# Attention and a Fourier mixing layer on one core: turned tiles and attention's outputs go through memory in fewer transfers, the second batch's outputs too

## The chip, the core and the metric

The kernel runs on one core of a Trainium2 chip. The core has a matrix engine (TensorE, PE in the profile; PEld are its weight loads), three engines for everything else (VectorE or DVE, ScalarE or ACT, GpSimd or POOL), and a sequencer, SyncE or SP, which here only issues transfers. Transfers run on 16 DMA engines between memory and the core's SBUF; PE writes to a small memory of its own, PSUM, from which DVE and ACT read. The metric is the device time in microseconds of one execution, as the median of several runs; a profile of one execution comes with it.

## The reference

For 4 batches, 8 heads, 768 rows and 64 columns per head, attention with a block mask (blocks of 32 rows: neighbours, the first and last block, and three drawn blocks per block row), and after it a Fourier mixing layer on the joined heads (4 x 768 x 512):

```python
scores = scale * np.matmul(q, k.transpose(0, 1, 3, 2))
scores = np.where(mask, scores, -1000000000.0)
attn = exp(scores - max) ; attn = attn / (sum(attn) + 1e-09)
x = (attn @ v).transpose(0, 2, 1, 3).reshape(B, S, H * D)

X = np.fft.fft(np.fft.fft(x, axis=1), axis=2)
u = x + np.real(X)
un = (u - mean(u)) / np.sqrt(var(u) + 1e-06)
out = u + np.maximum(un @ w_ch1, 0.0) @ w_ch2      # 512 -> 2048 -> 512
```

## The kernel before

The work is laid out by a planner written in Python: it emits the instructions of all engines in one order, and each engine then runs its own in that order, waiting by semaphores for what an instruction needs. The planner keeps an estimate of each engine's time (`when`), and decides by it where a step goes.

**Attention** goes in *slots*. A pair of heads (16 pairs, 4 per batch) has 6 slots; a slot takes two units of 128 keys for one half of the queries (384). For each unit PE makes the scores (`scores`, L578); ACT takes the exponential, and PE multiplies it by v one slot later (`values`, L652), adding into the one PSUM buffer `o`. The mask comes in one of two ways. As long as no channel products are waiting, PE adds it into the scores (L588, four products to a slot) and ACT writes `e` itself (L598). Later, ACT works in place (L606) and DVE multiplies by the mask (L608). Row sums are collected by additions on DVE (L633) or POOL (L638) and taken up by PE (L733, `sp`).

**An output** `o` of a pair and a half is turned, so that rows come to lie in partitions, and put into `x`, the input of the mixing layer. There are two ways. `place`: ACT copies `o` to `oT` (L663), PE turns it in three products with the identity (L675, `xt`), ACT copies the result into `x` (L676). `place_blocks`: DVE turns `oT` in blocks of 32 x 32 (L660), and SP puts the 16 blocks in place with 16 transfers from SBUF to SBUF (L691). `in_blocks` says which pairs take the second way: before, all of batches 2 and 3 but the first pair of each. `sum_p` holds one `oT`.

**The mixing** of a batch (`fourier`, `mixer`) starts when its attention is done and runs beside the next batch's attention: folds on DVE, products along the rows (`zp`, L856) and across (`pq`, L887 to L904) on PE, then per tile of 128 rows and per half `arrive` (L926), `spread` (statistics, L937), `whiten` (L951), which gives the normalised `un`. For the channel products `un` must be turned. In the last batch PE does that (L992). In the others `un_blocks` turns blocks of 32 x 32 on DVE (L1010) and writes them to memory (`far`, L1013, four transfers per tile of 128 x 512); when all six tiles of a batch are there, `un_back` fetches both halves into `unT` (L1022, four transfers per half). `unT` has two buffers in all.

**The channel products** follow. `right` makes four differences of `unT` on DVE (L1053); a `quad` then is seven products of the first weight (`xp`, `yp`, `z`, L1091) with sums on DVE (L1096) and a ReLU on ACT (L1100); `channels` multiplies by the second weight (`y`, L1147), adds into `x` (L1150) and stores it (L1158). They make up the greater part of PE's work and are spread over the attention of the next batch.

**What sets the order.** Steps of the mixing wait in the queue `apart`, channel products in `late`, short PE steps (turnings, totals) in `short`. `gap` emits steps from `apart` as far as the planner's times allow. A step of `right` (kind `"b"`) is to wait until `state["back"]`, which `un_back` sets to the planner's time plus `BACK` (9.0 us). But at the end of each slot from batch 2's attention on, a loop takes up to four steps from `apart` regardless, when fewer than 18 are left:

```python
for _ in range(4 if phase > 1 and not late and len(apart) < 6 * T else 0):
    if apart and not late:
        do_apart()
```

When the last step of `apart` is emitted, the channel products become available and the mask goes over from PE to DVE (`masks["by_pe"] = False`).

All transfers here are issued by SP, in order: loads of q (L230), k (L230) and v (L270), block transfers, `far` writes, fetches, stores. An issue that waits holds up the others behind it.

Of the kernel before, what the change touches and what calls it, by code (L numbers as in the profile page):

```python
# [11 lines left out]
FP32 = mybir.dt.float32  # L12
# [10 lines left out]
def _words(ap, n):  # L23

    return bass.DRamTensorHandle(ap.tensor.name, (2 * n,), I32)
# [74 lines left out]
def kernel(  # L100
# [14 lines left out]
    nc = tc.nc  # L115

    B, H, S, D = q.shape
    DM = H * D
    FF = w_ch1.shape[1]
    P = 128  # L120
    C = S // P
    BLK = 32
    NB = S // BLK
    NR = sampled_blocks.shape[1]
    HS = S // 2
# [4 lines left out]
    T = C // 2  # L130
# [4 lines left out]
    NP = H // 2  # L135
# [40 lines left out]
    xp = ctx.enter_context(tc.tile_pool(name="xp", bufs=2))  # L176
# [8 lines left out]
    far_p = ctx.enter_context(tc.tile_pool(name="far_p", bufs=1, space=bass.MemoryType.DRAM))  # L185
# [7 lines left out]
    when = {"PE": 0.0, "ACT": 0.0, "DVE": 0.0, "POOL": 0.0}  # L193
    free = {"m": [0.0, 0.0], "t": [0.0]}

    def busy(engine, us, after=0.0):
        when[engine] = max(when[engine], after) + us
        return when[engine]

    def bank(tag):  # L200

        at = free[tag].index(min(free[tag]))
        when["PE"] = max(when["PE"], free[tag][at])
        free[tag][at] = float("inf")
        return tag, at

    def give(which, at):
        free[which[0]][which[1]] = at + HOP
# [91 lines left out]
    def bit(n):  # L300
# [5 lines left out]
                      in_=bass.AP(tensor=_words(sampled_blocks, NB * NR), offset=0,  # L306
                                  ap=[[0, NB], [1, 2 * NB * NR]]))
# [135 lines left out]
    for w, w_sb in ((w_ch1, w1_sb), (w_ch2, w2_sb)):  # L443
        rows, cols = w.shape
# [45 lines left out]
    turned, e_of, acc_of, o_of, sums_of, x_of, sp_of = {}, {}, {}, {}, {}, {}, {}  # L490
# [176 lines left out]
    def place(n, half):  # L667

        b, j = pairs[n]
        oT = o_of.pop((n, half))  # L670
        if j == 0:
            x_of[b, half] = xp.tile([P, T, DM], FP32, tag=("xA", "xB")[half], name="x")
        xt, at = ps_t.tile([P, 512], FP32, tag="t", name="xt"), bank("t")
        for c in range(T):
            nc.tensor.transpose(xt[:, c * P:(c + 1) * P], oT[:, c * P:(c + 1) * P], ident)  # L675
        nc.scalar.copy(out=x_of[b, half][:, :, j * P:(j + 1) * P],  # L676
                       in_=xt[:, 0:HS].rearrange("p (c f) -> p c f", c=T))
        give(at, busy("ACT", 0.5, busy("PE", 0.45, oT_at[n, half]) + HOP))

    def in_blocks(n):  # L680

        return n > 2 * NP and n % NP > 0

    def place_blocks(n, half):
        b, j = pairs[n]
        oT = o_of.pop((n, half)).rearrange("p (c t d) -> p c t d", t=P // BLK, d=BLK)
        for g in range(P // BLK):
            for t in range(P // BLK):  # L690
                nc.sync.dma_start(  # L691
                    out=x_of[b, half][BLK * t:BLK * t + BLK, :, j * P + BLK * g:j * P + BLK * (g + 1)],
                    in_=oT[BLK * g:BLK * g + BLK, :, t, :])

    def into_sums(key, j, sp):
        if j == 0:
# [281 lines left out]
    def mixer(b, xA, xB):  # L978


        uns, unT = {}, {}
# [21 lines left out]
        lines = {}  # L1003

        def un_blocks(half, m):

            un = uns.pop((half, m))
            if half not in lines:
                lines[half] = far_p.tile([BLK, DM // BLK, HS], FP32, tag=f"un{half}", name="far")
            nc.vector.transpose(out=un, in_=un)  # L1010
            for g in range(P // BLK):
                n = m * P + g * BLK
                nc.sync.dma_start(out=lines[half][:, :, n:n + BLK],  # L1013
                                  in_=un[BLK * g:BLK * g + BLK, :].rearrange(
                                      "j (t i) -> j t i", i=BLK))

        def un_back():

            for half in range(2):
                unT[half] = tr_p.tile([P, ND, T * P], FP32, tag="tr", name="unT")  # L1020
                for a in range(P // BLK):
                    nc.sync.dma_start(out=unT[half][BLK * a:BLK * a + BLK, :, :],  # L1022
                                      in_=lines[half].rearrange(
                                          "j (k a) n -> a j k n", a=P // BLK)[a])
            state["back"] = max(when["PE"], state["ready"]) + BACK

        t, s = {}, {}
        K1, K2 = slice(0, ND // 2), slice(ND // 2, ND)
# [169 lines left out]
        def outputs(r, m, after):  # L1198
# [60 lines left out]
            if r == 1:  # L1259
# [5 lines left out]
              for h in range(2)]  # L1265

        ft = [[("d", lambda h=h, m=m: un_blocks(h, m), 0.0, 0.0, 0.7) for m in range(T)]
              for h in range(2)]

# [9 lines left out]
        if not last:  # L1279
            before = first + [pq[1], ar[0][1], ar[1][1], sp[0][1],  # L1280
                              pq[2], wh[0][1], ft[0][1], ar[0][2], ar[1][2], sp[0][2],
                              pq[0], wh[0][2], ft[0][2], ar[0][0], ar[1][0], sp[0][0],
                              sp[1][1], wh[0][0], ft[0][0], sp[1][2], wh[1][1], ft[1][1],
                              sp[1][0], wh[1][2], ft[1][2], wh[1][0], ft[1][0]]
            after = ([("-", un_back, 0.0, 0.0, 0.0)] + le +
                     [("b", lambda i=i: right(i, 0, 1, 2), 0.0, 0.0, 1.0) for i in (1, 2, 3, 4)])
# [5 lines left out]
        for r in range(0 if last else NF // 4):  # L1292
# [9 lines left out]
    MOST, LEAST = 9.6, 2.5  # L1302
    COVER = 100.0
    AHEAD = 2.2
    BACK = 9.0
    ALONE = 3.0
    LEAVES = 9.0
    SP = UP // SLOT
# [2 lines left out]
    short, apart, late, due = deque(), deque(), deque(), deque()  # L1311
    asked = set()
    needed = set()
    state = {"paired": False, "total": None, "w": 0, "got": 0, "owed": 0.0, "ready": 0.0,
             "back": 0.0}
# [9 lines left out]
    def do_apart():  # L1325
        kind, fn, pe, act, dve, _ = apart.popleft()
        if kind[0] in "dwb":
            dve += behind(kind)
            state["ready"] = busy("DVE", dve, {"w": rstd_at[0] if rstd_at else 0.0,
                                               "b": state["back"]}.get(kind, state["ready"])) + HOP  # L1330
            fn()
            return
        done = state["ready"]
        if kind != "-":
            at = bank(kind[0])
            done = busy("PE", pe, done) + HOP
        fn()
        if act:
            done = busy("ACT", act, done) + HOP
        if dve:  # L1340
            done = busy("DVE", dve, done) + HOP
        if kind != "-":
            give(at, done - HOP)
        state["ready"] = done
# [31 lines left out]
    def until(met):  # L1376

        while not met():
            if late:
                channel_step()  # L1380
                gap(2.0)
            else:
                do_apart()
# [35 lines left out]
    def slot(sl):  # L1419
        phase, r = divmod(sl, SB)  # L1420
        n, s = divmod(sl, SP)
# [48 lines left out]
        if s >= (5 if reuse else 3) and (n, 0) in oT_at and once(n):  # L1470
            b, j = pairs[n]
            at = oT_at[n, 0]
            if reuse:
                until(lambda: (b - 2, 0) in finished)
                at = when["PE"] + LEAVES
            if in_blocks(n):
                place_blocks(n, 0)
            else:
                short.append(("t", at, lambda: place(n, 0)))
        if 0 < sl <= B * SB and s == 0 and n % NP != 1:  # L1480
            if in_blocks(n - 1):
                place_blocks(n - 1, 1)
            else:
                short.append(("t", oT_at[n - 1, 1], lambda: place(n - 1, 1)))
        if sl < B * SB and n % NP == 1 and s == 1:
            b = pairs[n - 1][0]
            at = oT_at[n - 1, 1]
            if b >= 2:
                until(lambda: (b - 2, 1) in finished)
                at = when["PE"] + LEAVES  # L1490
            short.append(("t", at, lambda: place(n - 1, 1)))
        if sl > SB and s == 0 and sl <= B * SB:
            short.append(("t", acc_at[n - 1, 1], lambda: total(n - 1)))
            state["total"] = short[-1]
# [27 lines left out]
            gap(rest())  # L1522

        for _ in range(4 if phase > 1 and not late and len(apart) < 6 * T else 0):
            if apart and not late:
                do_apart()

        must = (3, 5) if paired else (2, 5)
# [5 lines left out]
        while short and (not more or soon) and (  # L1534
                s in must or len(short) > 1 or phase == 0 or soon or sl == B * SB):
            ready = [i for i in short if max(i[1], min(free[i[0]])) <= when["PE"] + 0.1]
# [36 lines left out]
    for sl in range(B * SB + 1):  # L1573
        slot(sl)
        if sl == B * SB - 4:
            flag = highest()
        if sl == B * SB - 2:
            over = nc.values_load(flag[0:1, 0:1], min_val=0, max_val=1)
# [107 lines left out]
```

## Time and profile before

| | |
|---|---|
| median of 3 runs | 1062.29 us (1061.61 to 1062.72) |
| the profiled execution's own time | 1060.62 us |
| its span, first to last instruction | 1058.8 us |
| PE busy | 1022.0 us (97%), 4334 instructions |
| DVE busy | 677.8 us (64%), 1236 |
| ACT busy | 356.5 us (34%), 718 |
| POOL busy | 241.6 us (23%), 272 |
| granted PE clock, mean | 0.991 |
| transfers | 55.72 MB in 162,017 packets, 146,572 of them under 512 bytes |
| L675, turning of outputs on PE | 60 products of 128 x 128, 11.0 us busy |
| L588, mask on PE | 200 products, 24.9 us busy |
| L660, turning on DVE | 12, 584 ns each |
| far<-un | 72 issues of 64 KB |
| unT<-far | 24 issues of 192 KB |
| x<-oT | 192 issues of 12 KB |

A line of a timeline is: start in us, duration, engine, line of the kernel, operation, what it writes and reads, the shape, how many were merged, and in brackets the idle time of the engine before it and what ended it. Where a wait is put down to a transfer, the name is that of a transfer that landed at about that time, and may be another than the one waited for. Between about 123 and 264 us attention of batch 1 runs beside the mixing of batch 0; batch 0's channel products, with batch 1's mixing, fill most of 264 to 414; batch 2's attention starts with slot 48 at 226 us and is then spread to 557; batch 3's attention runs from 542 to 786.

### The profile page before, as it was taken

How to read it: one execution, taken by the hardware profiler on the slowest of the kernel's cores; microseconds unless marked ns; L12 is line 12 of the kernel's file. 1: busy time of each engine (PE TensorE's matmuls, PEld its weight loads, DVE VectorE, ACT ScalarE, POOL GpSimd, SP SyncE). 2: the span in 40 equal slices, each digit the busy share in tenths (PEclk: the TensorE clock that was granted, in tenths of full speed). 3: DMA queues.
4: the chain of work that ended last, by engine and by line, in shares of the span. 5: the costliest groups of instructions: out<-in, count | busy, mean ns of one | idle time of the engine just before them, and what ended most of it. 6: DMA issues, size and time to landing. Idle time of an engine off the chain costs nothing.

```text
span 1058.8 us, 12480 instructions
## 1 busy us (share of the span) xinstructions
PE 1022.0 (97%) x4334; PEld 529.7 (50%) x4334; DVE 677.8 (64%) x1236; ACT 356.5 (34%) x718; POOL 241.6 (23%) x272
## 2 busy tenths in 40 slices
PE   8999999987999999999999999899999999999996
PEld 4333345433465554444444654344444654578575
DVE  6898795968754845564578466665457364674663
ACT  6988755553120112342441210253220211210210
POOL 1000183554200100554553001255520001000000
PEclk9999999998999999999999999999999999999999
DMA  7757422381000124222230003621000001000001
GB/s 214 230 170 225 108 46 46 50 147 28 1 0 11 20 44 96 57 38 44 41 56 1 1 11 60 134 43 27 12 10 5 1 1 37 24 1 1 1 16 47
DMA packets 162017, 55.72 MB, mean 53 GB/s; under 512 B 146572, under 2 KB 155034, under 8 KB 161946
## 3 DMA queue, kind: packets, MB, share of 16 engines
q1 hardware_dynamic: 160694, 54.11, 22.7%
q10 hardware_dynamic: 1220, 0.72, 0.3%
q8 instruction: 36, 0.59, 0.2%
q14 instruction: 35, 0.29, 0.1%
q0 software_dynamic: 32, 0.01, 0.0%
HBM read 41.44 MB, written 11.01 MB: 50 GB/s over the span
## 4 chain that ended last, share of the span: by engine, by line
PE 82%; DVE 6%; DMA 3%; ACT 3%; SPq 2%; issue 2%; POOL 0%; ACTq 0%; DVEq 0%
PE y L1147 22%; PE z L1091 15%; PE s L578 11%; PE o L652 9%; PE yp L1091 7%; PE yy L1212 7%; PE xp L1091 4%; PE zp L856 2%; PE sp L719 1%; DVE t L1053 1%; ACT e L598 1%; DMA kb<-in_k_dram 1%; PE s L588 1%; DMA out_dram<-x 1%; PE sp L733 1%
## 5 line engine op out<-in xcount | busy, mean ns | idle before, releaser
L638 POOL TENSOR_TENSOR acc<-acc,e 128x384 f32<-128x384 f32 x162 | 164.6, 1052 | 97.4 <-DVE e L608 81.1
L578 PE MATMUL s<-qT,kT 64*128 64x384 f32 x768 | 156.5, 523 | 20.4 <-DVE e L608 13.1
L652 PE MATMUL o<-e,vr 128*64 128x384 f32 x768 | 142.4, 498 | 0.0
L1147 PE MATMUL y<-w_sb,hB 128*128 128x512 f32 x288 | 128.6, 597 | 0.3 <-DVE x L1150 0.3
L1147 PE MATMUL y<-w_sb,hA 128*128 128x512 f32 x288 | 127.9, 595 | 0.0
L1150 DVE TENSOR_TENSOR x<-y,x 128x512 f32<-128x512 f32 x72 | 49.7, 691 | 111.7 <-PE y L1147 111.6
L608 DVE TENSOR_TENSOR e<-s,mask 128x768 f32<-128x768 f32 x92 | 83.8, 951 | 58.1 <-ACT s L606 49.9
L578 PEld LDWEIGHTS s<-qT,kT 64*128 64x128 f32 x768 | 64.4, 187 | 100.1 <-DVE e L608 28.0
L638 POOL TENSOR_TENSOR acc<-e 128x384 f32<-128x384 f32 x44 | 48.5, 1123 | 257.3 <-PE sp L733 127.2
L606 ACT ACTIVATE s<-s 128x768 f32<-128x768 f32 x92 | 70.0, 792 | 92.6 <-PE s L578 92.4
L1091 PE MATMUL z<-unT,t 128*128 128x384 f32 x256 | 93.2, 487 | 0.7 <-DVE hA L1096 0.7
L598 ACT ACTIVATE e<-s 128x768 f32<-128x768 f32 x100 | 76.0, 810 | 48.6 <-PE s L588 29.6
L1147 PEld LDWEIGHTS y<-w_sb,hB 128*128 128x128 f32 x288 | 53.6, 191 | 67.2 <-issue 65.7
L1147 PEld LDWEIGHTS y<-w_sb,hA 128*128 128x128 f32 x288 | 53.7, 190 | 63.7 <-issue 60.2
L652 PEld LDWEIGHTS o<-e,vr 128*64 128x64 f32 x768 | 48.1, 137 | 71.5 <-issue 68.0
L1096 DVE TENSOR_TENSOR hA<-z,hA 128x384 f32<-128x384 f32 x64 | 35.7, 557 | 68.5 <-PE z L1091 68.5
L1100 ACT ACTIVATE hA<-hA 128x384 f32<-128x384 f32 x64 | 33.4, 523 | 123.8 <-DVE hA L1096 123.8
L1091 PEld LDWEIGHTS z<-unT,t 128*128 128x128 f32 x256 | 48.5, 190 | 35.4 <-DVE hA L1096 2.0
L1100 ACT ACTIVATE hB<-hB 128x384 f32<-128x384 f32 x64 | 33.5, 523 | 86.2 <-DVE hB L1096 83.8
L1111 ACT COPY hA<-xp 128x384 f32<-128x384 f32 x32 | 15.3, 478 | 128.6 <-PE xp L1091 128.6
L1091 PE MATMUL yp<-unT,w_sb 128*128 128x384 f32 x128 | 46.7, 487 | 0.8 <-ACT hA L1111 0.6
L1091 PE MATMUL xp<-unT,w_sb 128*128 128x384 f32 x128 | 47.2, 492 | 0.0
(208 smaller groups left out, 1364.2 us busy)
## 6 DMA issues: line engine op xcount, KB each, us to landing
wraw<-in_moe_w_ch_dram SPq DMA_DIRECT2D x32, 512.0 KB
vr<-in_v_dram SPq DMA_DIRECT2D x30, 192.0 KB
far<-un SPq DMA_DIRECT2D x72, 64.0 KB
unT<-far SPq DMA_DIRECT2D x24, 192.0 KB
qb<-in_q_dram SPq DMA_DIRECT2D x44, 96.0 KB
kb<-in_k_dram SPq DMA_DIRECT2D x44, 96.0 KB
x<-oT SPq DMA_DIRECT2D x192, 12.0 KB
out_dram<-x SPq DMA_DIRECT2D x11, 252.0 KB
```

The lines of the kernel that those rows point to most:

```text
L578: nc.tensor.matmul(s[:, i, 0:HS], kT[rows, c * P:(c + 1) * P], qT[rows, queries], start=True, stop=u not in by_pe)
L598: nc.scalar.activation(out=e, in_=s[:, :, 0:HS], func=ACT.Exp, scale=scale)
L606: nc.scalar.activation(out=s[:, :, 0:HS], in_=s[:, :, 0:HS], func=ACT.Exp, scale=scale)
L608: nc.vector.tensor_tensor(out=e, in0=s[:, :, 0:HS], in1=m.broadcast_to([P, 2, HS]), op=ALU.mult)
L638: nc.gpsimd.tensor_add(out=acc[:, i, :], in0=start[:, i, :], in1=e[:, i, :])
L652: nc.tensor.matmul(o[D * i:D * i + D, :], vt[:, i, c, :], e[:, i, :], start=(c == 0), stop=(c == C - 1))
L1091: nc.tensor.matmul(to, a[:, k, :], c[:, k, :], start=(k == 0), stop=(k == ND // 2 - 1))
L1096: tt(out=to, in0=ps, in1=a, op=ALU.add)
L1100: nc.scalar.activation(out=h, in_=h, func=ACT.Relu)
L1147: nc.tensor.matmul(y, hs[0, half][:, l, m * P:(m + 1) * P], w2_sb[:, 4 * r + l, :], start=(l == 0), stop=(l == 3))
L1150: nc.vector.tensor_tensor(out=x[:, m, :], in0=y, in1=x[:, m, :], op=ALU.add)
L1212: nc.tensor.matmul(ps, a[:, k, :], c[k // 2][:, k % 2, :] if isinstance(c, list) else c[:, k, :], start=(k == 0), stop=(k == 3))
```

## The change

- `in_blocks` now also holds for the four pairs of batch 1.
- `place_blocks` goes through memory: four transfers write the blocks of `oT` into a tile `row` in memory, in pieces of 128 bytes, and four read it into `x`, in pieces of 512 bytes. The four reads wait until the writes have landed.
- `un_blocks` writes a turned tile to memory as it is, in one transfer of 256 KB (2 KB per row). `un_back`, still in four transfers per half, does the rearrangement on its way back, in pieces of 128 bytes instead of 1,536; 8 x 1,536 = 12,288 pieces to a batch.
- `BACK` is 13.0 for batch 0 and 12.0 for the others.
- The loop at the end of a slot leaves a step of `right` in the queue until `state["back"]` is near.

```diff
-        return n > 2 * NP and n % NP > 0
+        return NP <= n and (n < 2 * NP or n % NP > 0)

     def place_blocks(n, half):
         b, j = pairs[n]
-        oT = o_of.pop((n, half)).rearrange("p (c t d) -> p c t d", t=P // BLK, d=BLK)
+        rows = far_p.tile([BLK, T, P // BLK, P], FP32, tag=f"oT{half}", name="row", bufs=2)
+        oT = o_of.pop((n, half))
         for g in range(P // BLK):
-            for t in range(P // BLK):
-                nc.sync.dma_start(
-                    out=x_of[b, half][BLK * t:BLK * t + BLK, :, j * P + BLK * g:j * P + BLK * (g + 1)],
-                    in_=oT[BLK * g:BLK * g + BLK, :, t, :])
+            nc.sync.dma_start(
+                out=rows.rearrange("r c t f -> r (c t) f")[:, :, BLK * g:BLK * g + BLK],
+                in_=oT[BLK * g:BLK * g + BLK, :].rearrange("r (ct d) -> r ct d", d=BLK))
+        if j == 0:
+            x_of[b, half] = xp.tile([P, T, DM], FP32, tag=("xA", "xB")[half], name="x")
+        for t in range(P // BLK):
+            nc.sync.dma_start(
+                out=x_of[b, half][BLK * t:BLK * t + BLK, :, j * P:(j + 1) * P],
+                in_=rows[:, :, t, :])
...
-                lines[half] = far_p.tile([BLK, DM // BLK, HS], FP32, tag=f"un{half}", name="far")
+                lines[half] = far_p.tile([T, P, DM], FP32, tag=f"un{half}", name="far")
             nc.vector.transpose(out=un, in_=un)
-            for g in range(P // BLK):
-                n = m * P + g * BLK
-                nc.sync.dma_start(out=lines[half][:, :, n:n + BLK],
-                                  in_=un[BLK * g:BLK * g + BLK, :].rearrange(
-                                      "j (t i) -> j t i", i=BLK))
+            nc.sync.dma_start(out=lines[half][m], in_=un)
...
+                of = lines[half].rearrange("m (g j) (k a i) -> a j k (m g) i",
+                                           j=BLK, a=P // BLK, i=BLK)
                 for a in range(P // BLK):
-                    nc.sync.dma_start(out=unT[half][BLK * a:BLK * a + BLK, :, :],
-                                      in_=lines[half].rearrange(
-                                          "j (k a) n -> a j k n", a=P // BLK)[a])
-            state["back"] = max(when["PE"], state["ready"]) + BACK
+                    nc.sync.dma_start(
+                        out=unT[half][BLK * a:BLK * a + BLK].rearrange(
+                            "j k (g i) -> j k g i", i=BLK),
+                        in_=of[a])
+            state["back"] = max(when["PE"], state["ready"]) + BACK[b > 0]
...
-    BACK = 9.0
+    BACK = 13.0, 12.0
...
-            short.append(("t", at, lambda: place(n - 1, 1)))
+            if in_blocks(n - 1):
+                place_blocks(n - 1, 1)
+            else:
+                short.append(("t", at, lambda: place(n - 1, 1)))
...
-            if apart and not late:
+            if apart and not late and (apart[0][0] != "b" or
+                                       state["back"] < max(when["DVE"], when["PE"]) + 0.2):
                 do_apart()
```

## The prediction

> **What bounds the kernel now.** I read the page's busy shares first: TensorE (PE) 1022.0 of 1058.8 us, the chain of waits 82% PE. A saving must therefore take work off PE or fill a place where PE stands. The PE timelines show the two places that matter. The first is where batch 0's normalised rows come back from memory:
>
> ```profile
> 229.58 1.56 PE L578 MATMUL s<-qT,kT 64*128 64x384 f32 x8
> 230.97 0.49 PE L588 MATMUL s<-factors 64*128 64x384 bf16 x4
> 231.39 0.55 PE L675 MATMUL xt<-ident,oT 128*128 128x128 f32 x3
> 231.87 1.51 PE L652 MATMUL o<-e,vr 128*64 128x384 f32 x8
> ...
> 245.32 2.93 PE L578 MATMUL s<-qT,kT 64*128 64x384 f32 x8 [8.08 <-DVE e L608]
> ```
>
> The reader sees one slot of attention (scores L578, mask L588, a turned output L675, outputs L652), then PE standing 8.08 us for VectorE (DVE). The DVE timeline says why: it stands at the fetched tile `unT`, with everything behind it.
>
> ```profile
> 226.16 0.95 DVE L633 TENSOR_TENSOR acc<-acc,e 128x768 f32<-128x768 f32 x1
> 236.96 1.11 DVE L1053 TENSOR_TENSOR t<-unT 128x768 f32<-128x768 f32 x1 [9.85 <-DMA kb<-in_k_dram]
> ```
>
> The second place is batch 2's (ACT, DVE and PE timelines):
>
> ```profile
> 662.31 0.48 ACT L676 COPY x<-xt 128x384 f32<-128x384 f32 x1 [17.97 <-DMA out_dram<-x]
> ```
>
> ```profile
> 676.03 1.82 DVE L1053 TENSOR_TENSOR t<-unT 128x768 f32<-128x768 f32 x1 [3.93 <-DMA kb<-in_k_dram]
> ```
>
> ```profile
> 657.18 1.56 PE L578 MATMUL s<-qT,kT 64*128 64x384 f32 x8
> 664.54 2.79 PE L578 MATMUL s<-qT,kT 64*128 64x384 f32 x8 [3.06 <-DVE e L608]
> ...
> 692.68 1.78 PE L578 MATMUL s<-qT,kT 64*128 64x384 f32 x8 [1.14 <-DVE e L608]
> ```
>
> ScalarE (ACT) cannot place an output because the store that frees the tile is late in SP's queue; the exponentials behind it are late, and PE stands. Last, windows over 140-171, 184-223, 246.5-248.5 and 228-234 us (busy us and count of PE, PE loads, DVE, ACT, POOL, then clock, DMA share, GB/s):
>
> ```profile
> 140.00:171.00 31.00, 29.86 (x181) 13.27 (x177) 30.34 (x31) 17.48 (x34) 20.04 (x17) 1.00 0.21 39
> 184.00:223.00 39.00, 36.99 (x231) 16.57 (x231) 37.33 (x65) 20.29 (x44) 22.44 (x24) 1.00 0.39 67
> 246.50:248.50 2.00, 2.00 (x9) 0.66 (x6) 0.59 (x1) 1.00 (x2) 2.00 (x3) 0.55 0.98 158
> 228.00:234.00 6.00, 6.00 (x43) 2.42 (x39) 0.00 (x0) 4.58 (x8) 3.13 (x4) 1.00 1.04 215
> ```
>
> DVE is full in the first two (30.34 of 31, 37.33 of 39): while batch 0 is mixed, it has no room. The last two give the rate of 128-byte pieces (a q load, 158 GB/s) and of 1,536-byte pieces (the fetch, 215), both into 32 partitions.
>
> **The change, part by part.** Sums go against the profiled execution's 1060.62 us; the median 1062.29 stands 1.67 above it.
>
> (1) Batch 1's eight outputs leave PE: 24 transposes. A slot with one starts 138.86 and ends 142.60 (3.74), one without 135.60 to 138.86 (3.26). 8 x 0.47 = **-3.8**. With them 8 copies of L663 (480 ns) and 8 of L676 (484 ns) leave ACT, 34% busy: 0.
>
> (2) The order of the changed program starts batch 0's channel products after attention's slot 53 instead of between 51 and 53, and the mask stays on PE until then: 16 more L588, four slots. A slot with masks takes 3.26, one without 2.93 (259.81 to 262.74): 4 x 0.33 = **+1.3**. For these, DVE makes 8 sums (1044 ns) instead of 8 mask products (951 ns), POOL 16 additions fewer: 0, DVE being idle there.
>
> (3) The right-hand tiles (L1053) are no longer pushed onto DVE before they can have come. The 8.08 goes, and the slow stretch behind it (granted clock 0.55 in the row above: 2.93 for 1.56, and 0.4 at 254.3): **-9.9**. Late next are (4) and (5).
>
> (4) The eight turnings move to DVE, 584 ns each (L660). PSUM has one buffer `o`, so PE's next half of outputs waits until DVE has read the last. ACT did this at once; DVE has a queue. Walk along the rows of before: the first turning stands behind L633, which ends 142.5, so it ends 143.1, where PE would start its next L652 at 140.7: 2.4. The third stands before the L545 at 167.5, with 1.96 of L826-L828 moved behind it and three turnings ahead, 1.75, and 0.4 of a wait for a sum: 167.7, where PE would be at 164.2: 3.5. In 184-223, DVE's 39.5 us get four turnings (2.3), one sum (1.0) and 2.4 in which it waits for the last products of z, which PE reaches only after such a wait: 45.2, against 38.3 of PE's ten slots: 7.0. Together 12.9, less the 3.5 of like waits that stand there already (L578 and L675 on ACT): **+9.4**. Bounds: 0, if DVE's lag costs no more than it does now, and 12.9. I take the walk, because DVE's 30.34 of 31 is nearest to it.
>
> (5) The new wait for the first fetch. On SP, the last normalised tile and the fetch now stand behind a k load (4 issues, 2.2), four row writes (2.6), their landing, four reads into x (2.6); then one write of 256 KB (0.6). A transfer's fixed part is the fetch's 10.45 (issue 226.51 to 236.96) less 1.573 MB at 215 GB/s (7.3): 3.1, so the landing costs 2.5 after the issue ends. The fetch itself is 12,288 pieces of 128 bytes, at 158 GB/s 10.0 plus 3.1. Sum 23.6, of which 2.0 runs before DVE's last turned tile; two L1053 follow (2.7): 24.3 after it. PE gets there 18.3 after it (five slots 17.2, xp and yp 2.9, less 1.8 that it was ahead). **+6.0**, the first channel product z behind it, nothing else on DVE. Bounds: 0 (k load and row hop hidden), and 10.3 (reads at half of 215).
>
> First stretch: -3.8 + 1.3 - 9.9 + 9.4 + 6.0 = **+3.0**.
>
> (6) Batch 2. The same stretch of batch 1 takes 27.33 (414.56 to 441.89), this one 35.50: 8.17 is to be had. Each `far` write is one issue (0.6) instead of four (2.7, and 5.0 at 649.4), so the store ahead of ACT's copy is issued at about 655 and lands by 658, when PE has just turned (657.2): the 3.06 goes and what follows from it. The fetch is issued at 657.4 and lands at 657.4 + 13.1 = 670.5; L1053 stands one L1150 later, at 671.9. The second L1053 ends about 0.7 after PE wants it; half a microsecond stays at the next store. **-7.0**; bounds -8.2 and -2 (fetch late too).
>
> (7) At 0: batch 1's fetch (SP waits for PE to free `unT`; it lands near 409, L1053 comes after the third L1150, about 411.6; without that cover 2); 8 issues instead of 16 for outputs of batches 2 and 3 (7.9 us against 10.3, with nobody waiting); SP in batch 1, with 16 more issues per pair and a wait of 2.5 for each row: loads of v and q queue behind, but have over 10 us until their use.
>
> Sum +3.0 - 7.0 = -4.0: 1056.6, as a median **1058.3**. All low ends give 1041.7, all high ends 1071.1.
>
> A rule that speaks against the change: the Trainium skill, "DMA: Bandwidth & Descriptors", Specifications, says that a transfer reaches line rate only from 512 bytes per piece up. The two rates above (158 and 215) agree; by 215 for both, the sum would be 2.7 lower.
>
> **Rivals.**
> - *DVE keeps pace.* (4) is 0: POOL's adds lengthen DVE's instructions where both run (L803 0.76 to 1.23 us), and DVE idles from 170.9 to 183.7 but for 0.98, so slots may slide there. Against it: the two full windows. Sum -13.4: 1048.9.
> - *Slower: the fetch in small pieces.* The reads step through memory by 64 KB from piece to piece, which no load of before does; they could run below 158 GB/s. Each us more falls on the first fetch in full, on batch 2's after 1.4 of margin; it decides from 12.7 us for a fetch (124 GB/s) on. At 110 GB/s: 4.3 + 2.9 - 4.0 = +3.2, 1065.5. For it: nothing here reads so; against it: q loads at 158 with 8 KB steps.
> - *Batch 2 isn't mended.* The store is behind SP's other stores, or the fetch late: (6) is -2, the sum +1.0: 1063.3. Against it: SP's four-issue writes are what fill 649.4-654.4.
>
> **How the numbers follow.** Forecast 0.45 (own range 1054.5 to 1062), DVE keeps pace 0.25, small pieces 0.17, not mended 0.13. A measurement tells 0.2%, 2.1 us, from no change. Faster (below 1060.2): 0.33 of the first, all of the second, 0.58. Same: 0.10, 0.02 and 0.06, 0.18. Slower: 0.02, 0.15 and 0.07, 0.24. Range 1049 to 1066: half of the second case and the worst of the third stay out.
>
> **What would show it.** (1) no L675 between 130 and 235 us; (2) 216 L588; (3) no wait of about 8 us of L578 for L608; (4) L652 waiting for DVE's L660, some 9 us in all before 240; (5) one wait of 4 to 8 us of the first z product for L1053; (6) 27 to 29 us where batch 2 takes 35.5. Wrong if L652 hardly waits (then faster), or if a fetch takes over 13 us (then slower).

## The result, and the profile after

The changed kernel is slower: a median of 1067.03 us (1064.53 to 1068.09, 7 runs) against 1062.03 us for the kernel before on the same chip, a ratio of 1.0045 with a 95% interval of 1.0035 to 1.0056. Faster, 1058.3, was forecast. The profiled execution took 1065.39 us with a span of 1063.7; before it was 1060.62 and 1058.8. The two spans differ by 4.9, and the executions by about what the medians do (4.8 and 5.0), so the spans can be compared part by part. A part of a single profile has an uncertainty of its own: the start, where nothing was changed, differs by 0.7.

The parts are cut where a slot's scores begin on PE (slots counted from 0). In us:

| | before | after | difference | forecast |
|---|---|---|---|---|
| start to slot 24 | 123.08 | 122.40 | -0.7 | 0 |
| slot 24 to 55: batch 1's attention, first fetch | 295.70 | 302.68 | **+7.0** | +3.0 |
| slot 55 to 78 | 238.40 | 238.59 | +0.2 | 0 |
| slot 78 to 82: batch 2 | 38.65 | 37.16 | **-1.5** | -7.0 |
| slot 82 to the end | 362.97 | 362.87 | -0.1 | 0 |

The groups of the page show where PE now stands. After "|" come busy time and mean, then the idle time in front of the group and what ended most of it:

```profile
L652 PE MATMUL o<-e,vr 128*64 128x384 f32 x768 | 145.4, 507 | 8.6 <-DVE oT L660 8.5
L1096 PE MATMUL z<-t,w_sb 128*128 128x384 f32 x128 | 48.1, 500 | 6.4 <-DVE t L1058 6.3
```

The 8.08 us stop of before is gone. In its place stand 8.5 for turnings on DVE, and 6.3 for the differences of the fetched tiles of batches 0 and 2. The PE timeline gives the places in the first stretch, each wait in brackets:

```profile
142.43 1.51 PE L652 MATMUL o<-e,vr 128*64 128x384 f32 x8 [2.36 <-DVE oT L660]
...
168.05 2.83 PE L652 MATMUL o<-e,vr 128*64 128x384 f32 x8 [4.56 <-DVE oT L660]
...
224.41 2.32 PE L578 MATMUL s<-qT,kT 64*128 64x384 f32 x8 [2.38 <-ACT e L598]
...
256.26 1.53 PE L1096 MATMUL xp<-unT,w_sb 128*128 128x384 f32 x4 [0.79 <-DMA unT<-far]
...
263.76 2.90 PE L1096 MATMUL z<-t,w_sb 128*128 128x384 f32 x4 [4.67 <-DVE t L1058]
```

Look at the second number as well as the bracket: L652 takes 1.51 behind the first stop and 2.83 behind the second. Windows right behind the second and the third stop (the clock is the third number from the end) say why:

```profile
168.00:170.80 2.80, 2.75 (x8) 0.77 (x8) 2.70 (x3) 0.40 (x1) 0.00 (x0) 0.50 0.28 45
226.50:230.80 4.30, 3.57 (x14) 0.92 (x10) 4.17 (x7) 1.51 (x2) 0.47 (x2) 0.50 0.91 179
```

PE runs at half its clock there. The DVE timeline shows what the stop of 4.56 waits for: PE wants `o` free at 163.5, and the turning L660 stands behind these and one more that began before.

```profile
164.07 0.97 DVE L828 TENSOR_TENSOR e<-e 128x128 f32<-128x128 f32 x1
164.96 1.21 DVE L809 SCALAR_TENSOR_TENSOR sd<-sd,not_first 128x257 f32<-128x257 f32 x1
166.21 0.43 DVE L809 SCALAR_TENSOR_TENSOR sd<-sd 128x257 f32<-128x257 f32 x1
166.55 0.95 DVE L633 TENSOR_TENSOR acc<-acc,e 128x768 f32<-128x768 f32 x1
167.42 0.58 DVE L660 STREAM_TRANSPOSE oT<-o 128x384 f32<-128x384 f32 x1
```

In batch 2 the stop of 3.06 (before, at the scores of 664.54) is gone, but another, two slots later, has grown from 1.14 to 3.25. SP's queue follows, first before and then after; a line of SPq merges issues, from the start of the first to the end of the last:

```profile
665.78 5.16 SPq L1022 DMA_DIRECT2D unT<-far  x8
672.71 7.59 SPq L230 DMA_DIRECT2D kb<-in_k_dram  x4
```

```profile
664.59 9.95 SPq L1026 DMA_DIRECT2D unT<-far  x8
674.64 2.25 SPq L1163 DMA_DIRECT2D out_dram<-x  x3
676.94 6.91 SPq L230 DMA_DIRECT2D kb<-in_k_dram  x4
683.96 2.86 SPq L1163 DMA_DIRECT2D out_dram<-x  x6
```

ACT and PE after:

```profile
693.87 0.48 ACT L676 COPY x<-xt 128x384 f32<-128x384 f32 x1 [4.37 <-DMA out_dram<-x]
```

```profile
696.15 2.52 PE L578 MATMUL s<-qT,kT 64*128 64x384 f32 x8 [3.25 <-DVE e L608]
```

ACT's copy L676 waits for batch 1's last stores (L1163), which SP issues from 683.96 on, although DVE has had their last tile ready since 678.2. Ahead of them are a fetch that holds SP for 9.95 us and a k load that holds it for 6.91. The exponentials (L606) stand behind the copy.

### The profile page after: what moved, and what is told of

Its sections match the earlier page's. It is cut to its first block, busy times and chain, and to the rows that moved or that the text cites. A ratio compares the mean times of both kernels' runs of the same rounds, so it can differ in the third digit from the quotient of the medians.

```text
span 1063.7 us, 12373 instructions
## 1 busy us (share of the span) xinstructions
PE 1021.3 (96%) x4326; PEld 529.9 (50%) x4326; DVE 672.1 (63%) x1244; ACT 349.8 (33%) x702; POOL 220.2 (21%) x256
## 4 chain that ended last, share of the span: by engine, by line
PE 82%; DVE 6%; DMA 3%; SPq 3%; ACT 3%; issue 2%; POOL 0%; DVEq 0%; ACTq 0%
PE y L1152 23%; PE z L1096 15%; PE s L578 10%; PE o L652 9%; PE yp L1096 7%; PE yy L1217 7%; PE xp L1096 4%; PE zp L862 2%; PE sp L725 1%; ACT e L598 1%; PE s L588 1%; PE sp L739 1%; SPq L1026 1%; DMA out_dram<-x 1%; SPq L230 1%
## 5 line engine op out<-in xcount | busy, mean ns | idle before, releaser
L638 POOL TENSOR_TENSOR acc<-acc,e 128x384 f32<-128x384 f32 x150 | 149.6, 1032 | 101.0 <-DVE e L608 71.3
L578 PE MATMUL s<-qT,kT 64*128 64x384 f32 x768 | 155.0, 520 | 11.4 <-ACT e L598 6.9
L652 PE MATMUL o<-e,vr 128*64 128x384 f32 x768 | 145.4, 507 | 8.6 <-DVE oT L660 8.5
L578 PEld LDWEIGHTS s<-qT,kT 64*128 64x128 f32 x768 | 64.7, 188 | 92.2 <-ACT e L598 27.1
L608 DVE TENSOR_TENSOR e<-s,mask 128x768 f32<-128x768 f32 x84 | 76.5, 952 | 52.2 <-ACT s L606 43.7
L598 ACT ACTIVATE e<-s 128x768 f32<-128x768 f32 x108 | 82.0, 810 | 62.7 <-PE s L588 46.0
L638 POOL TENSOR_TENSOR acc<-e 128x384 f32<-128x384 f32 x40 | 42.1, 1073 | 246.9 <-ACT e L598 122.5
L606 ACT ACTIVATE s<-s 128x768 f32<-128x768 f32 x84 | 63.8, 792 | 87.3 <-PE s L578 86.9
L652 PEld LDWEIGHTS o<-e,vr 128*64 128x64 f32 x768 | 48.7, 138 | 82.0 <-issue 69.4
L1101 DVE TENSOR_TENSOR hA<-z,hA 128x384 f32<-128x384 f32 x64 | 35.7, 558 | 68.6 <-PE z L1096 68.6
L1096 PE MATMUL z<-t,w_sb 128*128 128x384 f32 x128 | 48.1, 500 | 6.4 <-DVE t L1058 6.3
```

The costliest lines, as they stand in the source:

```text
L578: nc.tensor.matmul(s[:, i, 0:HS], kT[rows, c * P:(c + 1) * P], qT[rows, queries], start=True, stop=u not in by_pe)
L598: nc.scalar.activation(out=e, in_=s[:, :, 0:HS], func=ACT.Exp, scale=scale)
L606: nc.scalar.activation(out=s[:, :, 0:HS], in_=s[:, :, 0:HS], func=ACT.Exp, scale=scale)
L608: nc.vector.tensor_tensor(out=e, in0=s[:, :, 0:HS], in1=m.broadcast_to([P, 2, HS]), op=ALU.mult)
L638: nc.gpsimd.tensor_add(out=acc[:, i, :], in0=start[:, i, :], in1=e[:, i, :])
L652: nc.tensor.matmul(o[D * i:D * i + D, :], vt[:, i, c, :], e[:, i, :], start=(c == 0), stop=(c == C - 1))
```

## The experiments

Three theories stood at first. **T1**: the turnings on DVE cost most of the first stretch, since DVE is the one that frees the PSUM buffer `o`. **T2**: the fetch in 128-byte pieces and SP's longer queue are the cost. **T3**: DVE merely has too much to do, and its backlog will stop PE in one place or another. All times are medians with the ratio to the kernel before on the same chip. "First" is slot 24 to 58 (321.74 us before, 328.91 after; up to slot 58, because in some kernels work moves among slots 53 to 57), "batch 2" is slot 78 to 84 (52.46 before, 50.97 after), both from the profiled execution. The expectations count otherwise: their "first stretch" is slot 24 to 55 (302.7 after) and their batch 2 is slot 78 to 82 (37.2 after). Line numbers shift from kernel to kernel: the products `xp`, `yp` and `z` stand at L1091 before and at L1090 to L1101 elsewhere, the differences of `unT` at L1053 before and at L1052 to L1063 elsewhere.

### Each part of the change alone, and all but one

**All but the turnings.** In the changed kernel:

```diff
-        return NP <= n and (n < 2 * NP or n % NP > 0)
+        return n > 2 * NP and n % NP > 0
```

> The changed kernel with one line undone: the outputs of batch 1 are turned by TensorE again (24 products L675), all else as changed. Theory T1 (turning on VectorE holds the one PSUM buffer `o`, so TensorE's L652 waits, 8.6 us, and each stop is followed by a slow clock): those waits and the 2.4 us wait of L578 at 222 go, the first stretch falls from 302.7 to 287 to 290 us, and the time is 5 to 9 us under the kernel before: 1053 to 1057. Theory T2 (the fetch in 128-byte pieces and SP's longer queue are what costs): L652's waits go, but the first product z comes as late as now and the first stretch stays within 3 us of 302; time 1062 to 1067.

1058.57 us, ratio 0.9969 (0.9956 to 0.9981); first 319.68, batch 2 50.85. L652 no longer waits, but only 9.2 of the 13 to 16 us that T1 forecast for the first stretch are gained: `z` now waits 3.4 us at 242 us for DVE's mask product, which stands behind the differences. The time lies between the ranges of T1 and T2. So the change without batch 1's turnings is faster than the kernel before, and they cost 0.76% net of the 24 products that they save: some 8 us. The edit takes their way through memory off SP too (the fetch is issued at 223.80 instead of 246.71), so these 8 us are T1 and the longer queue of T2 together; the later experiments separate them.

**Only the turnings**: `in_blocks`, `place_blocks` and its call as changed, all else as before.

```diff
-        return n > 2 * NP and n % NP > 0
+        return NP <= n and (n < 2 * NP or n % NP > 0)
...
-            short.append(("t", at, lambda: place(n - 1, 1)))
+            if in_blocks(n - 1):
+                place_blocks(n - 1, 1)
+            else:
+                short.append(("t", at, lambda: place(n - 1, 1)))
```

> The kernel before with the outputs of batch 1 turned by VectorE and sent through memory, and nothing else of the change. T1: L652 waits for L660 about 8 us before 240 us; 8 us of waits and 4 of slow clock less 3.7 for the 24 products that go: 1068 to 1072. T2: the turnings are hidden, -3.8: 1057 to 1060.

1080.18 us, ratio 1.0173 (1.0160 to 1.0187); first 339.81. L652's waits are there, 9.3 us before 245 us, as T1 has it, but the time is far worse than either theory expected. The PE and DVE timelines:

```profile
268.79 0.90 PE L752 MATMUL st<-ident,sums 128*128 128x128 f32 x3 [18.95 <-DVE sums L709]
```

```profile
266.32 0.96 DVE L1059 TENSOR_TENSOR t<-unT 128x768 f32<-128x768 f32 x1 [21.40 <-DMA unT<-far]
```

With the old loop, L1059 (L1053 of before) is pushed onto DVE early, and SP, with the row hops ahead, issues the fetch at 256.49 instead of 226.51 (a row hop is an output's way through memory: four writes, their landing, four reads). DVE stands for 21.40 us, and PE for 18.95. The later `BACK` with the loop's new condition is what keeps the changed kernel from this.

**Only the later `BACK`**, with the loop's condition.

```diff
-    BACK = 9.0
+    BACK = 13.0, 12.0
...
-            if apart and not late:
+            if apart and not late and (apart[0][0] != "b" or
+                                       state["back"] < max(when["DVE"], when["PE"]) + 0.2):
```

> The kernel before with only the later BACK and the loop's condition. Both theories: the 8.08 us stop and the slow clock after it go (9.9), four slots with masks on TensorE come (1.3): 1052 to 1056. If a wait for the fetch takes the stop's place, up to 6 us more: 1058 to 1060.

1062.21 us, ratio 1.0002 (0.9993 to 1.0011); first 322.32. The stop of 8.08 goes, and nothing is gained, which both theories missed. PE, then DVE:

```profile
246.56 1.56 PE L1091 MATMUL z<-t,w_sb 128*128 128x384 f32 x4 [1.46 <-DVE e L608]
...
252.72 2.37 PE L1091 MATMUL z<-unT,t 128*128 128x384 f32 x4 [3.31 <-DVE hA L1096]
```

```profile
243.89 1.75 DVE L1053 TENSOR_TENSOR t<-unT,t 128x768 f32<-128x768 f32 x1
245.56 1.81 DVE L608 TENSOR_TENSOR e<-s,mask 128x768 f32<-128x768 f32 x2
...
247.77 4.43 DVE L761 TENSOR_TENSOR x<-x,r 128x512 f32<-128x512 f32 x5
```

The channel products now start at once, and PE runs into DVE's own work, which the stop had sheltered: four differences of 1.7 us, the mask products and 4.43 us of batch 1's scaling. PE waits 4.8 there, and 1.76 at 413.8 for a copy of ACT that waits for a store; the slow clock comes twice.

**Only the memory layout**: `un_blocks` and `un_back`.

```diff
-            for g in range(P // BLK):
-                n = m * P + g * BLK
-                nc.sync.dma_start(out=lines[half][:, :, n:n + BLK],
-                                  in_=un[BLK * g:BLK * g + BLK, :].rearrange(
-                                      "j (t i) -> j t i", i=BLK))
+            nc.sync.dma_start(out=lines[half][m], in_=un)
...
-                    nc.sync.dma_start(out=unT[half][BLK * a:BLK * a + BLK, :, :],
-                                      in_=lines[half].rearrange(
-                                          "j (k a) n -> a j k n", a=P // BLK)[a])
+                    nc.sync.dma_start(
+                        out=unT[half][BLK * a:BLK * a + BLK].rearrange(
+                            "j k (g i) -> j k g i", i=BLK),
+                        in_=of[a])
```

> The kernel before with only the new memory layout of the turned tiles: one write of 256 KB per tile, and the fetch in 128-byte pieces. T1: the fetch takes 13 to 14 us instead of 10.45, VectorE stands at it about 3 us longer at 237 us, batch 2 gains 1 to 3 us: 1060 to 1064. T2: more than 4 us lost: 1066 or more.

1058.02 us, ratio 0.9961 (0.9948 to 0.9975); first 321.69, batch 2 51.28. That is faster than both ranges. The fetch holds SP for 10.19 us instead of 5.19, but as the writes ahead of it are shorter SP issues it at 223.59 instead of 226.51, so small pieces cost nothing in sum. That half of T2 falls; SP's longer queue, the other half, is not in this kernel. The stop of 3.06 goes here too, and one of 2.86 comes two slots later.

**All but the memory layout**: four writes per tile and the fetch in pieces of 1,536 bytes, with the rest as changed (the last diff the other way round, in the changed kernel).

> The changed kernel with the old memory layout of the turned tiles (four writes per tile, fetch in 1,536-byte pieces), the rest as changed. If the 4.64 us wait of the first product z is the fetch's length in small pieces (13 against 10.45 us) it falls by 2 to 3 us; as the old writes are four issues each, SP gets to the fetch 2 to 4 us later, and the wait stays at 4 to 6. In batch 2 the 3 us stop at the first score product comes back (38 to 39 us for the stretch). Time 1067 to 1070.

1071.97 us, ratio 1.0089 (1.0075 to 1.0103); first 332.26, batch 2 52.00. The fetch is shorter, but SP issues it at 259.72 instead of 246.71, behind four writes for each tile, and PE waits at once, for `xp` and not for the first `z`; the time is above the range:

```profile
266.08 2.90 PE L1097 MATMUL xp<-unT,w_sb 128*128 128x384 f32 x4 [6.79 <-DMA unT<-far]
```

### Who frees `o`

```diff
-            if in_blocks(n):
+            if in_blocks(n) and n < 2 * NP:
+                nc.scalar.copy(out=oT, in_=o_of.pop((n, half)))
+                nc.vector.transpose(out=oT, in_=oT)
+                oT_at[n, half] = busy("DVE", 0.5, busy("ACT", 0.5, when["PE"] + HOP) + HOP) + HOP
+            elif in_blocks(n):
                 nc.vector.transpose(out=oT, in_=o_of.pop((n, half)))
```

> The changed kernel, but for batch 1 ScalarE copies `o` out of PSUM (0.48 us, as L663 does) and VectorE then turns the copy in place: `o` is free without VectorE. T1 (the PSUM buffer held by a queueing VectorE): the waits of L652 for L660 (8.6 us) and the slow clock behind them (4) go; the wait for the first fetch stays or grows by up to 5, since TensorE gets there earlier; first stretch 291 to 297 us against 302.7, time 1056 to 1061. T3 (VectorE has simply too much to do until 255 us, and TensorE meets its backlog in another place): L578 waits for ScalarE's exponentials, which wait for VectorE's sums (as at 222 us), and the first stretch stays at 300 or more; time 1064 to 1067.

1063.00 us, ratio 1.0001 (0.9990 to 1.0013); first 325.42, which is 3.5 less than after. PE's waits from 123 to 256 us of the changed kernel (each: line, what it waited for, us in total, times, longest):

```profile
PE o L652 <- DVE oT L660: 8.5, 4, 4.6
PE s L578 <- ACT e L598: 2.9, 2, 2.4
```

and of this kernel:

```profile
PE s L578 <- ACT e L598: 6.7, 5, 2.7
PE xp L1100 <- DMA unT<-far: 3.4, 1, 3.4
```

T1 and T3 are both right in part. The 8.5 go, so the buffer was the cause of those. Then 3.8 come back as waits for exponentials, which wait for DVE's sums, and PE, which is there earlier, waits 3.4 for the fetch at `xp` and 3.5 at `z` (0.8 and 4.7 in the changed kernel), although it is issued 3.9 earlier (242.80 instead of 246.71). From slot 24 to 53 the kernel gains 6.5 us (129.74 to 123.20), and the fetch takes half of it away again.

### The late store in batch 2

First, batch 1's stores from ACT's queue:

```diff
-                store(half, m)
+                store(half, m, queue=nc.scalar if b == 1 else nc.sync)
```

> The changed kernel with batch 1's stores issued from ScalarE's queue instead of SP's, so that they don't stand behind the fetch and the k load. If the 3.25 us stop of L578 at 692.9 us comes from the store that SP issues late: the stop falls below 1 us and batch 2's stretch from 37.2 to 33 to 34.5 us; time 1062 to 1065. If it comes from the stores' own landing (rows on few DMA engines) or from the fetch sharing the DMA engines, the stop stays at 2.5 to 4 us and the time at 1066 to 1068.

1075.28 us, ratio 1.0122 (1.0108 to 1.0137); batch 2 57.51. The stop behind the store goes, as it should, but a worse one comes, which nobody expected:

```profile
667.82 21.06 SPq L1026 DMA_DIRECT2D unT<-far  x8
```

```profile
694.70 2.90 PE L1096 MATMUL z<-t,w_sb 128*128 128x384 f32 x4 [10.43 <-DVE t L1058]
```

Stores and fetch now run at the same time, and SP needs 21.06 us, from the first issue to the last, for a fetch that takes 9.95 without them. Together with the edit that frees `o` early it is the same:

> The two edits before last together (ScalarE frees `o` in batch 1; batch 1's stores from ScalarE's queue). T1 with the late store: the gains add up, 1052 to 1058, under both kernels. T3: 1062 to 1065.

1069.84 us, ratio 1.0067 (1.0053 to 1.0081); batch 2 58.92, a wait of 11.1 us for the fetch, and outside both ranges.

Then the order on SP alone: the k load of one pair comes two slots later, behind the stores.

```diff
-        if s == 0 and 0 < n < len(pairs) - 1:
+        if s == (2 if n == 3 * NP + 1 else 0) and 0 < n < len(pairs) - 1:
             load_k(n + 1)
```

> The changed kernel with one k load (of the pair after batch 3's second, at 677 us) issued two slots later, so that SP issues batch 1's last stores ahead of it. If the 3.25 us stop at 692.9 us comes from the last stores standing 7 us behind that k load on SP: L676 is no longer late, the stop goes with the slow clock behind it, batch 2's stretch falls from 37.2 to 32 to 34 us, time 1062 to 1064. If it comes from the store's landing alone (126 pieces of 2 KB, two at a time, 7 to 9 us), the stop stays at 2 us or more and the time at 1065 to 1068.

1062.62 us, ratio 1.0003 (0.9992 to 1.0014); batch 2 **45.63**, 6.8 less than before and 5.3 less than after. (Its first stretch, where nothing was changed, took 332.05: xp and z wait 6.8 there instead of 5.5, with more slow clock. A single profile's first stretch is uncertain by that much, and the medians decide.) SP's queue and ACT:

```profile
668.55 9.54 SPq L1026 DMA_DIRECT2D unT<-far  x8
678.19 7.25 SPq L1163 DMA_DIRECT2D out_dram<-x  x9
```

```profile
693.50 0.48 ACT L676 COPY x<-xt 128x384 f32<-128x384 f32 x1 [0.31 <-DMA out_dram<-x]
```

The copy now waits 0.31 instead of 4.37, PE stands nowhere between 686 and 700 us, and L578 behind it takes 1.56 instead of 2.52. The store theory holds. The same edit on three other kernels:

> The same edit on the kernel with batch 1's outputs turned by TensorE (which took 1058.57). By the store theory the 3.36 us stop goes there too: 1053 to 1056. Otherwise 1057 to 1060.

1052.77 us, ratio 0.9906 (0.9891 to 0.9922); batch 2 45.66.

> The same edit on the kernel before with the new memory layout alone (which took 1058.02). By the store theory the 2.86 us stop goes: 1053 to 1056. Otherwise 1057 to 1060.

1054.18 us, ratio 0.9920 (0.9907 to 0.9934); batch 2 46.23.

> The same edit on the kernel in which ScalarE frees `o` (which took 1063.0). By the store theory 1058 to 1060; if so, the two repairs add up, and what then still stands against the kernel before is the turnings on VectorE and the wait for the first fetch. Otherwise 1062 to 1064.

1058.49 us, ratio 0.9961 (0.9947 to 0.9974); batch 2 45.63. The two repairs, each worth 0.42 to 0.44%, add up to 0.84%. And on the kernel before:

> The kernel before with only the k load two slots later. The first stop of batch 2 (3.06 us, from the four-issue writes) stays and the second (1.14 us) goes: 1060 to 1062. If the k load was the cause of both: 1054 to 1057, as with the new layout.

1059.75 us, ratio 0.9979 (0.9970 to 0.9988); batch 2 49.85. The 3.06 stays and the 1.14 goes. So the new layout and the place of the k load are needed together: 6.2 to 6.8 us with both, 2.6 with the k load alone, 1.2 with the layout alone.

### What makes the first fetch late

Both kernels here start from the one that took 1058.49. Its queue on SP:

```profile
234.18 2.33 SPq L230 DMA_DIRECT2D kb<-in_k_dram  x4
236.61 2.87 SPq L695 DMA_DIRECT2D row<-oT  x4
241.00 2.50 SPq L701 DMA_DIRECT2D x<-row  x4
243.53 0.58 SPq L1021 DMA_DIRECT2D far<-un  x1
244.16 10.48 SPq L1030 DMA_DIRECT2D unT<-far  x8
```

First, the k load of pair 9 from ACT's queue (`load_blocks` is edited to issue on the queue that it is given):

```diff
-            load_blocks(n, 1, ld.tile([P, S], FP32, tag="k", name="kb"))
+            load_blocks(n, 1, ld.tile([P, S], FP32, tag="k", name="kb"),
+                        nc.scalar if n == 2 * NP + 1 else nc.sync)
```

> The kernel that took 1058.49 (ScalarE frees `o`, the later k load), with the k load that stands ahead of the first fetch issued from ScalarE's queue. If SP's queue sets the fetch, it is issued 2.4 us earlier and the waits of xp and z (7.0 us together) fall to 4 to 5: 1055 to 1057. If ScalarE's issues delay the exponentials, or the fetch is set by the last normalised tile, nothing is gained: 1058 to 1060.

1056.79 us, ratio 0.9951 (0.9938 to 0.9965); first 324.68 against 325.49. The fetch is issued 1.7 us earlier, at 242.49, and the first z starts 1.5 earlier. xp's wait falls from 3.6 to 1.1, while z's grows from 3.5 to 5.4, since xp and yp now run at full clock; 0.7 is lost to a wait for ScalarE's exponentials. The k load is a small part of it.

Then no row hops there: the outputs of batch 1's last pair are turned by PE.

```diff
-        return NP <= n and (n < 2 * NP or n % NP > 0)
+        return NP <= n and (n < 2 * NP - 1 or n >= 2 * NP and n % NP > 0)
```

> The kernel that took 1058.49 with the two outputs of batch 1's last pair turned by TensorE again, so that SP has no row hops between the last normalised tiles and the fetch. If the row hop (four writes, their landing, four reads, 5 to 7 us on SP) is what makes the fetch late, the fetch is issued 4 to 7 us earlier, the waits of xp and z (7.0) fall to 1 to 3, six products cost 1: 1052 to 1056. If the fetch is set by the last tile instead: 1057 to 1060.

1049.56 us, ratio 0.9887 (0.9871 to 0.9903), **12.1 us under the kernel before** and the fastest of all; first 316.70. SP, and PE at the first products:

```profile
232.05 2.19 SPq L230 DMA_DIRECT2D kb<-in_k_dram  x4
234.98 0.34 SPq L1021 DMA_DIRECT2D far<-un  x1
235.37 12.31 SPq L1030 DMA_DIRECT2D unT<-far  x8
```

```profile
253.61 1.53 PE L1100 MATMUL z<-t,w_sb 128*128 128x384 f32 x4 [1.13 <-DVE t L1062]
```

The fetch is issued at 235.37 instead of 244.16, and 7.1 us of waits (`xp` 3.59, `z` 3.51) become 1.1. With the row hop SP issued the last normalised tile 7.2 us after DVE had turned it (236.37 to 243.53), without it at once (234.95 to 234.98); the other 1.4 us of the 8.8 are DVE's, which is ready earlier. So the row hop made the fetch late, with the k load (1.7 in the run above) as a small part; the pieces are the same in both kernels. SP's longer queue, the half of T2 that was still open, was thus part of the cost.

## Why the prediction was wrong

Its sum was -4.0, and the spans differ by +4.9. The miss of 8.9 is 4.0 in the first stretch and 5.5 in batch 2, less 0.7 at the start, where nothing was changed. By its own steps:

1. **24 products off PE, -3.8**: right. PE's time for `xt` from slot 24 to 55, from each product's start to the next one's, falls from 4.7 us (30 products) to 0.9 (the other six).
2. **Four more slots with masks, +1.3**: right, 216 L588 in all.
3. **The first-fetch stop, -9.9**: gone as forecast, with its slow clock. But it is a saving only in this company. Alone it is worth nothing (1.0002), since DVE's own work is late next; on top of the turnings it is worth 0.8% (1.0173 against 1.0089). The step named (4) and (5) as what is late next; DVE's own work it did not name.
4. **Turnings on DVE, +9.4**: the mechanism was right, and was mis-sized. What is left of the +7.0 after the other steps is 7.0 + 3.8 - 1.3 + 9.9 - 7.0 = 12.4. L652's waits are 8.5, and "some 9 us in all" was forecast; the first two stops stand where the walk put them (2.4 forecast and 2.36 measured, 3.5 and 4.56). Two things failed. The walk took off 3.5 for waits of L578 and L675 that stand there already; they did not go: those of L578, without the 8.1, were 3.0 before and are 2.9 after, one of them (2.38) new. And no slow clock stood behind the stops in the walk: two L652 at 2.83 instead of 1.51 and two L578 at 2.32 and 2.40 instead of 1.56, with a mask, make 4.6, where before products were lengthened by 1.2 in these slots, apart from their waits. That is 9.2 of waits, with 0.8 ahead of the row sums (L739), and 3.4 of lengthened products: 12.6, within what the parts can be read to. The price of a stop had been worked out in step 3, 8.08 and 1.8, and was not carried to step 4.
5. **The first fetch, +6.0**: right within 1.0. 7.0 measured, the waits of 0.79 and 4.67 and 1.5 of slow clock. The chain on SP was the right reason, as the last experiment shows; inside it, the fetch took 14.95 us from its issue to the first L1058, where 13.1 was forecast. (The upper bound of 10.3 belongs to 110 GB/s; half of 215 gives 10.7.)
6. **Batch 2, -7.0**: this step failed. In its own window it gave 32.5 where 27 to 29 was forecast, and 1.5 of it were lost again in the slots behind. The first stop went, by the reason given, and the fetch landed for 678.9 with a wait of 1.59. What failed is "half a microsecond stays at the next store". It stayed 3.25: the fetch holds SP for 9.95 us and not for 5.2, as the eight issues of before do; then a k load of 6.91 us (7.59 before, so the row was there to be read; the last section says what holds it up) stands ahead of the last stores. With the k load behind the stores the stretch gives -6.8: what was to be had was right, and the queue behind the removed stop was not walked.
7. **The rest, 0**: right within 0.2.

Of the rivals, "batch 2 isn't mended" came true, for nearly the reason it gave (the store behind SP's other issues, a fetch and a k load, where it named other stores), together with steps 4 and 5 at 4.0 above their sum. Its 1063.3 fell short because it was priced with all else at the forecast. "The fetch in small pieces" gave 1065.5, close to the result by luck: the fetches ran at 148 and 144 GB/s and not at 110, and the layout alone gains (0.9961). "DVE keeps pace" is refuted by the 8.5 of L652. Of the two conditions under which the prediction called itself wrong, one came true: the fetches took 14 to 15 us, over 13; these one or two us are the smaller part of the miss.

The rule from the Trainium skill, "DMA: Bandwidth & Descriptors", Specifications (line rate from 512 bytes per piece), agrees in its direction: over the two fetches the windows of 247 to 259 and 665 to 678 us moved 148 and 144 GB/s, against 215 for 1,536-byte pieces before. It did not decide the result.

## What to carry to other kernels

When a wait is taken away, follow every queue behind it to the next thing that is late, with the work that the wait had sheltered and the issues that stand ahead of the next store; here one k load that was issued too early hid a gain of 5 us. Before a step is moved to an engine that is full, ask which buffer the engine then holds: a copy by an idle engine that frees the buffer can be worth more than the instruction that it costs. A round trip through memory is short on the DMA engines and long on the queue that waits for it, so keep it away from the fetch that the critical engine needs next.

## What the runs showed of the hardware that was not expected

- **A transfer in small pieces holds the queue that issues it.** Eight issues of the fetch take SP 5.16 us in pieces of 1,536 bytes, 9.5 to 12.3 in pieces of 128, and 21.06 with stores under way. SP was priced at 0.6 per issue.
- **Some stores run on two DMA engines, and what is issued right behind them is held up.** A store of 2 x 63 rows runs alone from 1034 to 1038 us in the changed kernel (last two numbers: share of 16 engines, GB/s):

```profile
1034.00:1038.00 4.00, 4.00 (x20) 3.54 (x19) 1.27 (x3) 0.00 (x0) 0.00 (x0) 1.00 0.13 43
```

  0.13 of 16 is two engines; a write of 128 rows shows 0.85 and 328 GB/s from 643.1 to 643.9. The Trainium skill, "DMA: Bandwidth & Descriptors", in the section on why a DMA increments its semaphore by 16, says that the number of engines is the largest up to 16 that divides the size of the slowest dimension on both sides; for the 2 of 2 x 63 that is two, and the trace agrees. In the 17 kernels of this document a k load follows right behind such a store (with one store of a single row between) 22 times, and takes SP 6.6 to 8.2 us; right behind stores of 64 rows it takes 2.35 to 2.46, three times, as in the kernel with the later `BACK` alone:

```profile
411.21 2.35 SPq L230 DMA_DIRECT2D kb<-in_k_dram  x4
```

  Elsewhere it takes 2.0 to 2.7, and 3.2 to 4.5 right behind a fetch. So the hold-up goes with the shape of the store. That the pieces for those two engines are what holds up the k load, and the fetch in the run with stores on ACT's queue, fits these numbers and was not tested.
- **The clock can drop after a stop of about 2 us.** In the 17 traces, from 100 to 1000 us, every stop of PE of 3.2 us or more was followed by a granted clock of 0.50, and none of 1.7 or less. Between these some were and some were not: the stop of 2.36 at 140 left the changed kernel at full speed, and the same one (2.37) in the kernel with the later k load was followed by 0.50, as was one of 1.76 at 413.8 with the later `BACK` alone. The Trainium skill, "TensorE: Matmul & The Clock Gate", Part 1, gives an idle window of about 3.4 us for it; here stops of half that were followed by it, so a stop is not safe because it is below that figure.
- **DVE's differences of `unT` take 0.95 us when POOL is idle and 1.09 to 1.75 when POOL adds.** In the kernel without batch 1's turnings on DVE, POOL's additions (L638) run for 8.88 us from 235.1 on, and the four differences from 238.35 to 244.8 take 6.6 us instead of 3.8, ahead of the mask product for which PE stands. In the fastest kernel POOL adds until 254.3, and the second and third difference take 1.63 and 1.75, the fourth, at 255.06, 0.94. It was seen, not tested.
